# An adaLN attention block on one core: 1/sigma broadcast through a DRAM row, scale parts by column tiles

## The chip, the cores and the metric

The kernel runs on one core of a Trainium2 chip. The metric is device time in microseconds (us) of one execution. The kernel before was run three times: 97.16 us in the median (97.13 to 97.92). The profile that this text reads is one further execution.

## The reference

Only these lines matter; `x` is 2 x 256 x 1152, all data bf16.

```python
mod = (_silu(c) @ w_mod).reshape(B, 6, 1, D)
shift_a, scale_a, gate_a, shift_m, scale_m, gate_m = [mod[:, i] for i in range(6)]
h = _layernorm(x, axis=-1) * (1 + scale_a) + shift_a
qkv = h @ wqkv
q, k, v = (qkv[..., :D].copy(), qkv[..., D:2 * D].copy(), qkv[..., 2 * D:].copy())
p = _softmax(jnp.einsum('bqd,bkd->bqk', q, k) * D ** (-0.5), axis=-1)
a = jnp.einsum('bqk,bkd->bqd', p, v) @ wo
return x + gate_a * a
```

So there are three modulation rows of 1152 values for each of the two batch entries (shift, scale, gate), a layer norm over 1152 columns, the three projections, attention over 256 keys with a single head, and the gated output projection.

## The kernel before, in words

**Layout.** The 512 tokens are four tiles of 128 (`t` = 0..3), the 1152 model columns nine tiles of 128 (`k` = 0..8). `x` is loaded with tokens on partitions, centred by its mean, and turned by TensorE (PE) into `xcT[k]`: model columns on partitions, 512 tokens along the row. All engines' instructions go through a recorder (`_Rec`), which is why nearly every line of the profile says L85, and at the end each engine's instructions, DMA issues included, are pinned to the order in which the program wrote them. What an engine does next is thus set by hand.

**Scale and normalisation are split.** `hTs[k] = xcT[k] * (1 + scale)` needs only the scale row; 1/sigma is multiplied in later. For K this is enough: a key's 1/sigma is applied to the scores in the end (`scores`, line 540), and the shift's share of K adds the same amount to all scores of a query, which the softmax drops. So the K projection starts from `hTs`, before the variances are known, and Q and V use `hT[k] = hTs[k] * rstd_bc + shift`, where `rstd_bc` is 1/sigma of the 512 tokens on all 128 partitions. `normalised(k)` (line 424) is the multiply on VectorE (DVE), `shifted(i)` (line 469) adds the shift row, two of three on DVE and one of three on ScalarE (ACT).

**Scale parts.** The scale row is computed in parts `PA`, `PB`, `PC` of the nine column tiles (line 41), as their weights `wS` arrive. `scale_rows` (line 270) makes the 128 columns of `wS` the stationary operand and silu(c), repeated to 32 columns, the moving one, so the result lies with model columns on partitions; `scale_out` adds 1 and `scaled_b` makes `hTs`. Every part costs nine matmuls for each of its column tiles. The shift row (lines 460 to 467) is made the other way round: silu(c) is the stationary operand of 32 columns, the weights `wH` move, and four matmuls each fill 32 PSUM partitions (a column tile of the array each); a DVE 32x32 block transpose then brings the columns to the partitions.

**K projection.** `accs[0..4]` are five PSUM banks that hold K's column tiles 0 to 4 while `k_step(k)` adds one row tile after the other. Tiles 5 to 8 have no bank of their own: their first two row tiles are computed early by `pair_part`, parked in `held` by `park`, and the rest comes in `held_block(i, ...)`, with `add_held(i)` adding the two on DVE. The named banks `pa`, `pb`, `pc` are shared by `psS`, the pairs, the transposes, `psK` and `psH`.

**1/sigma.** Variances come from DVE's batch-norm statistics for tiles 0 and 3 and from ACT's squares for 1 and 2; GpSimd (POOL) gathers them in `var` and takes the power -1/2 (lines 405 to 408). To bring `rstd` from one value per partition to a row on all partitions it is split in three bf16 parts, turned by PE (`pT3`), multiplied by a 12-row mask on DVE (`masked`), summed over the 12 rows by a matmul against ones (`bc_ps`) and copied to `rstd_bc` by ACT. This chain stands between the K steps on PE, and the nine `normalised` multiplies on DVE stand right behind it.

**Loads.** All weights are issued by SyncE (SP) in one order: `x`, parts of `wS`, the nine row tiles of `wK`, `wH`, `wQ`, `wG`, the rest of `wQ`, `wV`, `wO`. ACT issues only the load of `c` and the last store.

**The end.** In the output projection the last 192 columns of the last token tile use weights already multiplied by the gate (`wo_last`). The nine multiplies `gated_columns` are shared: `ONPOOL` = 4 on POOL (line 608), the other five on DVE, one after each chunk of the output from the fourth chunk on. DVE also does two operations for each chunk (`ga`, `o_sb`), and the last stores wait for its `o_sb`.

Of the kernel before, what the change touches and what calls it, by code (L numbers as in the profile page):

```python
# [16 lines left out]
def kernel(  # L17
# [20 lines left out]

    NACC = 5
    NPARK = KT - NACC  # L40
    PA, PB, PC = (0, 2), (2, 5), (5, KT)
    KA = PA[1]
    NR = 32

# [10 lines left out]
    work = ctx.enter_context(tc.tile_pool(name="work", bufs=2))  # L55
    const = ctx.enter_context(tc.tile_pool(name="const", bufs=1))
    small = ctx.enter_context(tc.tile_pool(name="small", bufs=4))
    psum = ctx.enter_context(tc.tile_pool(name="psum", bufs=5, space=PSUM))
    psum_a = ctx.enter_context(tc.tile_pool(name="psum_a", bufs=1, space=PSUM))
    psum_b = ctx.enter_context(tc.tile_pool(name="psum_b", bufs=1, space=PSUM))  # L60
# [5 lines left out]
    def bank(shape, name, dtype=None, where=None):  # L66
        if where is None:
            where = ring[turn_no[0] % len(ring)]
            turn_no[0] += 1
        return where[0].tile(shape, dtype or F32, tag=where[1], name=name)  # L70
# [39 lines left out]
    def one(t):  # L110
        return slice(t * P, (t + 1) * P)
# [8 lines left out]
    )  # L120
    neg_half = const.tile([P, TT], F32)
    gps.memset(neg_half, -0.5)
    NP3 = 3 * TT
    mask = const.tile([NP3, TT, P], BF16)

    gps.memset(mask, 1.0)
    gps.affine_select(
        out=mask, in_=mask, compare_op=ALU.is_ge, fill=0.0, base=0,
        pattern=[[-3, TT], [0, P]], channel_multiplier=1,
    )  # L130
    gps.affine_select(
        out=mask, in_=mask, compare_op=ALU.is_ge, fill=0.0, base=2,
        pattern=[[3, TT], [0, P]], channel_multiplier=-1,
    )

    c_sb = const.tile([P, B, KT], BF16)
    x_sb = act.tile([P, TT, D], BF16)
    sca.preload_act_table_set("natural_log_exp_and_others")
# [17 lines left out]
    def load_k(k0, k1, c0=0, c1=D):  # L156
        spq.dma_start(out=wK[:, k0:k1, c0:c1], in_=wqkv_v[:, k0:k1, D + c0 : D + c1])
# [21 lines left out]
    load_s(PC, 0, 4)  # L179
    load_s(PC, 4, KT)  # L180
    load_k(5, 6)
    load_k(6, 7)
    load_k(7, KT)
    for k0, k1 in ((0, 3), (3, 6), (6, KT)):
# [23 lines left out]


    mean = const.tile([P, TT], F32)  # L210
    var = const.tile([P, TT], F32)
    rstd = const.tile([P, TT], F32)
    nmean = const.tile([P, TT], F32)
    xc = act.tile([P, TT, D], BF16, tag="a1")
# [6 lines left out]
    def bn(t, after_second=None):  # L221
        st = small.tile([P, NCH, 6], F32, tag="stats", name="stats")
        for s in range(NCH):
            bn_part(t, st, s)
            if s == 1 and after_second is not None:
                after_second()
        mv = small.tile([P, 2], F32, tag="mv", name="mv")
        vec.bn_aggr(out=mv, in_=st)
        return mv

    def act_mean(t):
        sca.activation(out=xc[:, t, :], in_=x_sb[:, t, :], func=ACT.Copy, accum_out=ssum[t])
        sca.activation(out=nmean[:, t : t + 1], in_=ssum[t], func=ACT.Copy, scale=-1.0 / D)

    def act_var(t):
        sca.activation(out=xc[:, t, :], in_=x_sb[:, t, :], func=ACT.Square, bias=nmean[:, t : t + 1],
                       scale=1.0, accum_out=ssum[t])
        gps.tensor_scalar_mul(out=var[:, t : t + 1], in0=ssum[t], scalar1=1.0 / D)

    def centre(t, scalar, op, c0=0, c1=D):  # L240
        vec.tensor_scalar(out=xc[:, t, c0:c1], in0=x_sb[:, t, c0:c1], scalar1=scalar, scalar2=None, op0=op)
# [4 lines left out]
    def transposes(t, h, where):  # L246
        k0, k1 = HALF[h]
        tp = bank([P, 5, P], "tp", BF16, where)
        for k in range(k0, k1):
            ten.transpose(tp[:, k - k0, :], xc[:, t, k * P : (k + 1) * P], ident)  # L250
        tps[t, h] = tp
# [18 lines left out]
    def scale_rows(part, kk0, kk1, js=None, where=None):  # L270
        if kk0 == 0:
            psS[part] = bank([P, part[1] - part[0], NR], "psS", where=where)
        for j0, j1 in [part] if js is None else js:
            for kk in range(kk0, kk1):
                for j in range(j0, j1):
                    ten.matmul(psS[part][:, j - part[0], :], lhsT=wS[:, kk, j * P : (j + 1) * P], rhs=sc_rhs(kk),
                               start=(kk == 0 and j == part[0]), stop=(kk == KT - 1), skip_group_check=True)

    def scale_out(part):
        vec.tensor_scalar_add(out=s1p[:, part[0] : part[1], :], in0=psS[part][:, :, 0:B], scalar1=1.0)  # L280

    def scaled(k, sl, scalar):
        vec.tensor_scalar(out=hTs[:, k, sl], in0=xcT[:, k, sl], scalar1=scalar, scalar2=None, op0=ALU.mult)

# [4 lines left out]
    def scaled_b(k, b):  # L289
        scaled(k, tok(b), s1p[:, k, b : b + 1])  # L290
# [4 lines left out]
    def k_part(k, sl):  # L295
        for f in range(NACC):
            ten.matmul(accs[f][:, sl], lhsT=wk(k, f), rhs=hTs[:, k, sl],
                       start=(k == 0 and sl.start == 0), stop=False, skip_group_check=True)
# [7 lines left out]
            ten.matmul(ps[:, i, :], lhsT=wk(k, f0 + i), rhs=hTs[:, k, sl],  # L306
                       start=(k == 0 and i == 0), stop=(k == KA - 1), skip_group_check=True)

    def park(pr):
        ps, f0, sl = pr  # L310
        sca.copy(out=held[:, f0 - NACC : f0 - NACC + 2, sl], in_=ps)

    def k_step(k, f0=0, f1=NACC):
        for f in range(f0, f1):
            ten.matmul(accs[f], lhsT=wk(k, f), rhs=hTs[:, k, :],
                       start=False, stop=(k == KT - 1), skip_group_check=True)
# [9 lines left out]
    def add_held(i):  # L326
        vec.tensor_tensor(out=qkT[:, KT + NACC + i, :], in0=psK[i], in1=held[:, i, :], op=ALU.add)

    def evac(on_dve, out_ap, in_ap):
        if on_dve:  # L330
            return vec.tensor_copy(out=out_ap, in_=in_ap)
        return sca.copy(out=out_ap, in_=in_ap)


    fillers(12)
    sca.activation(out=e_sb, in_=c_sb, func=ACT.Exp, scale=-1.0)
    gps.tensor_scalar_add(out=e_sb, in0=e_sb, scalar1=1.0)
    mv0 = bn(0, after_second=silu_c)
    centre(0, mv0[:, 0:1], ALU.subtract)
    act_mean(1)  # L340
    centre(1, nmean[:, 1:2], ALU.add)
    act_mean(2)
    transposes(0, 0, MM)
    transposes(0, 1, MM)
    xcT_copy(0, 0, True)
# [45 lines left out]
    st3 = small.tile([P, NCH, 6], F32, tag="stats", name="stats")  # L391
    bn_part(3, st3, 0)
    act_var(1)
    for k in range(KA):
        k_part(k, one(3))
    scale_rows(PB, 0, KT, where=BA)
    scale_out(PB)
    for k in range(*PB):
        for b in range(B):
            scaled_b(k, b)  # L400
    bn_part(3, st3, 1)
    bn_part(3, st3, 2)
    mv3 = small.tile([P, 2], F32, tag="mv", name="mv")
    vec.bn_aggr(out=mv3, in_=st3)
    pr11, pr21 = pair(0, 1, BB), pair(1, 1, BC)
    for pr in (pr11, pr21):
        for k in range(KA):
            pair_part(pr, k)
        park(pr)
    act_var(2)  # L410
    gps.tensor_copy(out=var[:, 0:1], in_=mv0[:, 1:2])
    gps.tensor_copy(out=var[:, 3:4], in_=mv3[:, 1:2])
    gps.tensor_scalar_add(out=rstd, in0=var, scalar1=EPS)
    gps.tensor_tensor(out=rstd, in0=rstd, in1=neg_half, op=ALU.pow)
    for k in range(*PB):
        k_step(k)


    scale_rows(PC, 0, KT, where=BB)
    scale_out(PC)  # L420
    for k in range(*PC):
        for b in range(B):
            scaled_b(k, b)
    parts = const.tile([P, TT, 3], BF16)
    rest = const.tile([P, TT], F32)
    gps.tensor_copy(out=parts[:, :, 0], in_=rstd)
    gps.tensor_tensor(out=rest, in0=rstd, in1=parts[:, :, 0], op=ALU.subtract)
    gps.tensor_copy(out=parts[:, :, 1], in_=rest)
    gps.tensor_tensor(out=rest, in0=rest, in1=parts[:, :, 1], op=ALU.subtract)
    gps.tensor_copy(out=parts[:, :, 2], in_=rest)  # L430
    held_block(0, PB, BA)
    k_step(PC[0])
    k_step(PC[0] + 1, 0, 1)
    pT3 = bank([NP3, P], "pT3", BF16, BC)
    ten.transpose(pT3, parts.rearrange("p t i -> p (t i)"), ident)
    masked = const.tile([NP3, TT, P], BF16)
    vec.tensor_tensor(out=masked, in0=pT3.unsqueeze(1).to_broadcast([NP3, TT, P]), in1=mask, op=ALU.mult)
    k_step(PC[0] + 1, 1)
    bc_ps = bank([P, T], "bc_ps", where=BC)
    ten.matmul(bc_ps, lhsT=junk[:NP3, :P], rhs=masked.rearrange("p t n -> p (t n)"), start=True, stop=True)  # L440
    sca.copy(out=rstd_bc, in_=bc_ps)

    def normalised(k):
        vec.tensor_tensor(out=hT[:, k, :], in0=hTs[:, k, :], in1=rstd_bc, op=ALU.mult)

    for k in range(KT):
        normalised(k)
    for k in range(PC[0] + 2, KT):
        k_step(k)
    for f in range(NACC):  # L450
        evac(False, qkT[:, KT + f, :], accs[f])

    held_block(0, PC)
    held_block(1, (KA, KT), BC)
    held_block(2, (KA, KT), MM)
    add_held(0)
    add_held(1)


    psH = bank([P, KT, 32], "psH", where=BB)  # L460
    wH_v = wH.rearrange("p kk (k j c) -> p kk k j c", k=KT, j=4)
    for kk in range(KT):
        for j in range(4):
            ten.matmul(psH[32 * j : 32 * j + 32], lhsT=sc_rhs(kk), rhs=wH_v[:, kk, :, j, :],
                       start=(kk == 0), stop=(kk == KT - 1))
    shT = const.tile([P, KT, 32], F32)
    vec.transpose(out=shT.rearrange("p k c -> p (k c)"), in_=psH.rearrange("p k c -> p (k c)"))

# [9 lines left out]
    for i in range(KT * B):  # L478
        shifted(i)
    held_block(3, (KA, KT), BA)  # L480
    add_held(2)
    add_held(3)

    def wq(k, f):
        return wQ[:, k, f * P : (f + 1) * P]
# [119 lines left out]
        eng.tensor_tensor(out=wo_last[:, k, :], in0=wO[:, k, D - TAILW :],  # L605
                          in1=gate_bc[:, B - 1, D - TAILW :], op=ALU.mult)

    ONPOOL = 4
    for k in range(KT - ONPOOL, KT):
        gated_columns(gps, k)  # L610

# [85 lines left out]
```

## Time and profile before

| | |
|---|---|
| median of the runs | 97.16 us |
| the profiled execution's own time | 97.31 us |
| its span (first to last instruction) | 95.6 us |
| PE busy | 90.3 us (94% of the span), 661 matmuls |
| DVE busy | 69.4 us (73%) |
| ACT busy | 35.0 us (37%) |
| POOL busy | 23.2 us (24%) |
| TensorE clock granted | 1.000 |
| moved by DMA | 21.31 MB; the DMA engines are filled from about 2.5 to 52 us |

An entry of the time line gives the start in us from the span's start, the time that the merged instructions cover, the engine, the operation, output and input, how many there are, and in brackets how long the engine was idle before and what ended that. Matmuls overlap, so the step from one to the next is shorter than the duration of one. The time of 97.31 us is 1.7 us longer than the span; that part lies outside the instructions.

### The profile page before, as it was taken

Reading aid. Unit: us, or ns where it says so; the run is one execution under the profiler, and the core shown is the slowest. Engines: PE = TensorE matmul, PEld = TensorE weight load, DVE = VectorE, ACT = ScalarE, POOL = GpSimd, SP = SyncE. Lnnn points to the kernel's source line nnn. Section 1 sums busy time; section 2 is a strip of 40 time slices with the busy share of each in tenths; the row PEclk is TensorE's granted clock in tenths of the full one; section 3 lists DMA queues with packets and bytes.
Section 4 is the critical chain, followed back from the end, with each engine's and each line's share of the span. In section 5 each row is a group of like instructions: output and inputs, shape, how many; then the busy total and the mean of one; then the engine's idle time right before and its main releaser. Section 6 shows DMA issues by size and latency. Waiting matters only on the chain.

```text
span 95.6 us, 1687 instructions
## 1 busy us (share of the span) xinstructions
PE 90.3 (94%) x661; PEld 53.9 (56%) x665; DVE 69.4 (73%) x132; ACT 35.0 (37%) x73; POOL 23.2 (24%) x30
## 2 busy tenths in 40 slices
PE   3999999899999999999999999999999999999960
PEld 1349994633445444444458666556678656656660
DVE  2478868073999979999974899991018487999970
ACT  5197689002820900642330489233246300000020
POOL 5520002740000000000000000007999990018000
PEclk9999999999999999999999999999999999999999
DMA  2999999999999999999999102110000000311041
GB/s 28 336 328 358 372 401 380 408 414 408 406 404 411 412 410 412 385 372 371 391 413 409 73 0 52 36 29 0 0 0 0 0 0 0 130 67 57 10 185 52
DMA packets 16023, 21.31 MB, mean 223 GB/s; under 512 B 2192, under 2 KB 9360, under 8 KB 16016
## 3 DMA queue, kind: packets, MB, share of 16 engines
q1 hardware_dynamic: 15600, 21.19, 60.2%
q8 instruction: 5, 0.08, 0.3%
q10 hardware_dynamic: 416, 0.02, 0.3%
q14 instruction: 2, 0.02, 0.0%
HBM read 19.76 MB, written 1.18 MB: 219 GB/s over the span
## 4 chain that ended last, share of the span: by engine, by line
PE 76%; DMA 15%; SPq 3%; DVE 1%; issue 1%; ACT 0%
PE ps L85 41%; PE psQ L85 18%; DMA wS<-in_w_mod_dram 10%; PE psK L85 6%; DMA x_sb<-in_x_dram 5%; PE acc L85 5%; PE s_ps L85 4%; SPq L85 3%; PE psH L85 1%; PE psS L85 1%; DVE hTs L85 1%; PE bc_ps L85 0%; ACT o_sb L85 0%; DVE s1p L85 0%; PE pT L85 0%
## 5 line engine op out<-in xcount | busy, mean ns | idle before, releaser
L85 POOL PARTITION_ALL_REDUCE gate_bc<-gacc x2 | 13.7, 6886 | 44.5 <-DVE gacc L85 44.5
L85 DVE SCALAR_TENSOR_TENSOR gacc<-wG,scT_f,gacc 128x1152 f32<-128x1152 bf16 x16 | 22.4, 1416 | 0.4
L85 PE MATMUL ps<-wV,hT 128*128 128x384 bf16 x108 | 17.7, 326 | 0.0
L85 PE MATMUL psQ<-hT,wQ 128*128 128x512 bf16 x80 | 17.6, 379 | 0.1
L85 PE MATMUL ps<-wO,attnT 128*128 128x384 bf16 (+2 forms) x108 | 17.0, 319 | 0.0
L85 PEld LDWEIGHTS <-attnT 128*128 128x128 bf16 x126 | 11.4, 98 | 6.3
L85 PEld LDWEIGHTS <-hT 128*128 128x128 bf16 x108 | 10.6, 98 | 6.9
L85 PEld LDWEIGHTS <-wK 128*128 128x128 bf16 x109 | 9.5, 97 | 7.6 <-issue 1.0
L85 PEld LDWEIGHTS <-wQ 128*128 128x128 bf16 x81 | 7.9, 98 | 9.5
L85 PE MATMUL acc<-hTs,wK 128*128 128x512 bf16 (+2 forms) x64 | 11.0, 312 | 0.2
L85 ACT CAST qkT<-psQ 128x512 bf16<-128x512 f32 x9 | 5.0, 592 | 11.7 <-PE psQ L85 11.1
L85 DVE CAST attnT<-ps 128x512 bf16<-128x512 f32 (+1 forms) x6 | 3.5, 602 | 6.8 <-PE ps L85 6.8
L85 ACT CAST v_sb<-ps 128x384 bf16<-128x384 f32 x12 | 5.5, 475 | 7.9 <-PE ps L85 7.9
L85 DVE TENSOR_TENSOR ga<-ps,gate_bc 128x384 f32<-128x384 f32 (+2 forms) x12 | 6.4, 536 | 2.1 <-PE ps L85 2.0
L85 DVE TENSOR_TENSOR o_sb<-ga,x_sb 128x384 bf16<-128x384 f32 (+2 forms) x12 | 7.1, 595 | 0.4
L85 PE MATMUL junk_ps<-junk 128*128 128x512 bf16 x12 | 5.3, 632 | 1.5 <-DVE junk L85 1.5
L85 ACT CAST o_sb<-ps 128x128 bf16<-128x128 f32 (+1 forms) x2 | 0.5, 239 | 17.0 <-DVE ga L85 17.0
L85 DVE TENSOR_TENSOR hT<-hTs,held 128x512 bf16<-128x512 bf16 x9 | 5.5, 682 | 1.5 <-ACT held L85 1.5
L85 PE MATMUL psK<-hTs,wK 128*128 128x512 bf16 x26 | 6.3, 379 | 0.1
L85 DVE BATCH_NORM_STATS2 stats<-x_sb 128x6 f32<-128x384 bf16 x6 | 3.1, 541 | 2.2 <-DMA x_sb<-in_x_dram 2.2
L85 PEld LDWEIGHTS <-junk 128*128 128x128 bf16 (+1 forms) x13 | 1.7, 140 | 4.7 <-issue 3.2
L85 POOL TENSOR_TENSOR wo_last<-wO,gate_bc 128x192 bf16<-128x192 bf16 x4 | 2.5, 651 | 6.8 <-issue 6.8
(74 smaller groups left out, 89.7 us busy)
## 6 DMA issues: line engine op xcount, KB each, us to landing
wH<-in_w_mod_dram SPq DMA_DIRECT2D x3, 864.0 KB, 11.7
wG<-in_w_mod_dram SPq DMA_DIRECT2D x3, 864.0 KB, 12.7
wV<-in_wqkv_dram SPq DMA_DIRECT2D x3, 864.0 KB, 13.3
wO<-in_wo_dram SPq DMA_DIRECT2D x3, 864.0 KB, 8.7
wK<-in_wqkv_dram SPq DMA_DIRECT2D x7, 288.0 KB, 7.1
wQ<-in_wqkv_dram SPq DMA_DIRECT2D x3, 576.0 KB, 12.7
x_sb<-in_x_dram SPq DMA_DIRECT2D x4, 288.0 KB, 3.6
wQ<-in_wqkv_dram SPq DMA_DIRECT2D x1, 864.0 KB, 12.7
```

The costliest lines, as they stand in the source:

```text
L85: r = fn(*a, **k)
```

## The change

1/sigma no longer passes through PE. POOL computes `rstd` straight from the variances (now one tile `mvs`, which bn_aggr and ACT's squares write in place), ACT stores it to a DRAM row of 512 values, and a second DMA, issued by ACT as well, reads the row back to all 128 partitions (`rstd_all`, 128 x 2048 bytes); ACT copies it to `rstd_bc`, in another order of its elements. The mask, the three parts, `pT3`, `masked` and `bc_ps` go.

`PC` is cut in two (`PC` = tiles 5 and 6, `PD` = 7 and 8), with the loads of `PD` behind the load of wK's row tile 5. `PB`, `PC` and `PD` are computed by column tiles as the shift row is, with a DVE transpose each (`scale_tiles`, `scale_turned`); they stand at other places between the K steps. The shift row is made in two pieces with `held_block(2)` between them. One of the four parks and two of the five evacuations of `accs` move from ACT to DVE. The nine `normalised` move behind those evacuations and `add_held(0)`; `add_held(1)` moves behind `shifted`. `ONPOOL` becomes 2.

```diff
-    PA, PB, PC = (0, 2), (2, 5), (5, KT)
+    PA, PB, PC, PD = (0, 2), (2, 5), (5, 7), (7, KT)
...
     load_k(5, 6)
+    load_s(PD, 0, 4)
+    load_s(PD, 4, KT)
     load_k(6, 7)
...
     def act_var(t):
-        sca.activation(out=xc[:, t, :], in_=x_sb[:, t, :], func=ACT.Square, bias=nmean[:, t : t + 1],
-                       scale=1.0, accum_out=ssum[t])
-        gps.tensor_scalar_mul(out=var[:, t : t + 1], in0=ssum[t], scalar1=1.0 / D)
+        sca.activation(out=xc[:, t, :], in_=x_sb[:, t, :], func=ACT.Square, bias=snm[:, t : t + 1],
+                       scale=float(D) ** -0.5, accum_out=mvs[:, t, 1:2])
...
+    wS_v = wS.rearrange("p kk (k j c) -> p kk k j c", k=KT, j=4)
+    sT = const.tile([P, KT, 32], F32)
+    def scale_tiles(part, where):
+        psS[part] = bank([P, part[1] - part[0], 32], "psS", where=where)
+        for kk in range(KT):
+            for j in range(4):
+                ten.matmul(psS[part][32 * j : 32 * j + 32], lhsT=sc_rhs(kk), rhs=wS_v[:, kk, part[0] : part[1], j, :],
+                           start=(kk == 0), stop=(kk == KT - 1))
+    def scale_turned(part):
+        vec.transpose(out=sT[:, part[0] : part[1], :].rearrange("p k c -> p (k c)"),
+                      in_=psS[part].rearrange("p k c -> p (k c)"))
+        vec.tensor_scalar_add(out=s1p[:, part[0] : part[1], :], in0=sT[:, part[0] : part[1], 0:B], scalar1=1.0)
...
-    for k in range(KA):
-        k_part(k, one(3))
-    scale_rows(PB, 0, KT, where=BA)
-    scale_out(PB)
+    k_part(0, one(3))
+    scale_tiles(PB, BA)
+    k_part(1, one(3))
+    scale_turned(PB)
...
-        park(pr)
+        park(pr, on_dve=(pr is pr21))
     act_var(2)
-    gps.tensor_copy(out=var[:, 0:1], in_=mv0[:, 1:2])
-    gps.tensor_copy(out=var[:, 3:4], in_=mv3[:, 1:2])
-    gps.tensor_scalar_add(out=rstd, in0=var, scalar1=EPS)
+    gps.tensor_scalar_add(out=rstd, in0=mvs[:, :, 1], scalar1=EPS)
     gps.tensor_tensor(out=rstd, in0=rstd, in1=neg_half, op=ALU.pow)
-    for k in range(*PB):
-        k_step(k)
-    scale_rows(PC, 0, KT, where=BB)
-    scale_out(PC)
+    rstd_row = dram.tile([P, TT], F32, name="rstd_row")
+    rstd_all = const.tile([P, P, TT], F32)
+    sca.dma_start(out=rstd_row, in_=rstd)
+    sca.dma_start(out=rstd_all.rearrange("q p t -> q (p t)"),
+                  in_=rstd_row.rearrange("p t -> (p t)").partition_broadcast(P))
+    k_step(2)
+    k_step(3)
+    k_step(4, 0, 2)
+    scale_tiles(PC, BB)
+    scale_turned(PC)
     for k in range(*PC):
         for b in range(B):
             scaled_b(k, b)
...
+    k_step(4, 2)
     held_block(0, PB, BA)
-    k_step(PC[0])
-    k_step(PC[0] + 1, 0, 1)
-    pT3 = bank([NP3, P], "pT3", BF16, BC)
-    ten.transpose(pT3, parts.rearrange("p t i -> p (t i)"), ident)
...
-    bc_ps = bank([P, T], "bc_ps", where=BC)
-    ten.matmul(bc_ps, lhsT=junk[:NP3, :P], rhs=masked.rearrange("p t n -> p (t n)"), start=True, stop=True)
-    sca.copy(out=rstd_bc, in_=bc_ps)
+    k_step(5)
+    k_step(6, 0, 2)
+    scale_tiles(PD, BB)
+    scale_turned(PD)
+    for k in range(*PD):
+        for b in range(B):
+            scaled_b(k, b)
+    k_step(6, 2)
+    held_block(0, PC)
+    sca.copy(out=rstd_bc.rearrange("q (t p) -> q t p", p=P), in_=rstd_all.rearrange("q p t -> q t p"))
...
+    for k in range(*PD):
+        k_step(k)
+    for f in range(NACC):
+        evac(f < 2, qkT[:, KT + f, :], accs[f])
+    held_block(0, PD)
+    add_held(0)
     for k in range(KT):
         normalised(k)
-    for k in range(PC[0] + 2, KT):
-        k_step(k)
-    for f in range(NACC):
-        evac(False, qkT[:, KT + f, :], accs[f])
-    held_block(0, PC)
     held_block(1, (KA, KT), BC)
-    held_block(2, (KA, KT), MM)
-    add_held(0)
-    add_held(1)
...
+    shift_tiles(0, 6)
+    held_block(2, (KA, KT), MM)
+    shift_tiles(6, KT)
...
     held_block(3, (KA, KT), BA)
-    add_held(2)
-    add_held(3)
+    for i in (1, 2, 3):
+        add_held(i)
...
-    ONPOOL = 4
+    ONPOOL = 2
```

More of the change, by code (lines that the diff above doesn't have):

```diff
@@ L57 @@
     small = ctx.enter_context(tc.tile_pool(name="small", bufs=4))
+    dram = ctx.enter_context(tc.tile_pool(name="dram", bufs=1, space=bass.MemoryType.DRAM))
     psum = ctx.enter_context(tc.tile_pool(name="psum", bufs=5, space=PSUM))
@@ L122 @@
     gps.memset(neg_half, -0.5)
[L123 to L134, printed above, removed]
     c_sb = const.tile([P, B, KT], BF16)
@@ L210 @@
     mean = const.tile([P, TT], F32)
-    var = const.tile([P, TT], F32)
+    mvs = const.tile([P, TT, 2], F32)
+    snm = const.tile([P, TT], F32)
     rstd = const.tile([P, TT], F32)
@@ L226, in bn @@
                 after_second()
-        mv = small.tile([P, 2], F32, tag="mv", name="mv")
-        vec.bn_aggr(out=mv, in_=st)
-        return mv
+        vec.bn_aggr(out=mvs[:, t, :], in_=st)
     def act_mean(t):
@@ L307, in pair_part, with evac, park @@
                        start=(k == 0 and i == 0), stop=(k == KA - 1), skip_group_check=True)
-    def park(pr):
+    def evac(on_dve, out_ap, in_ap):
+        if on_dve:
+            return vec.tensor_copy(out=out_ap, in_=in_ap)
+        return sca.copy(out=out_ap, in_=in_ap)
+    def park(pr, on_dve=False):
         ps, f0, sl = pr
-        sca.copy(out=held[:, f0 - NACC : f0 - NACC + 2, sl], in_=ps)
+        evac(on_dve, held[:, f0 - NACC : f0 - NACC + 2, sl], ps)
     def k_step(k, f0=0, f1=NACC):
@@ L327, in add_held @@
         vec.tensor_tensor(out=qkT[:, KT + NACC + i, :], in0=psK[i], in1=held[:, i, :], op=ALU.add)
[L329 to L332, printed above, removed]
     fillers(12)
@@ L337 @@
     gps.tensor_scalar_add(out=e_sb, in0=e_sb, scalar1=1.0)
-    mv0 = bn(0, after_second=silu_c)
-    centre(0, mv0[:, 0:1], ALU.subtract)
+    bn(0, after_second=silu_c)
+    centre(0, mvs[:, 0, 0:1], ALU.subtract)
     act_mean(1)
@@ L342 @@
     act_mean(2)
+    gps.tensor_scalar_mul(out=snm[:, 1:3], in0=nmean[:, 1:3], scalar1=float(D) ** -0.5)
     transposes(0, 0, MM)
@@ L402 @@
     bn_part(3, st3, 2)
-    mv3 = small.tile([P, 2], F32, tag="mv", name="mv")
-    vec.bn_aggr(out=mv3, in_=st3)
+    vec.bn_aggr(out=mvs[:, 3, :], in_=st3)
     pr11, pr21 = pair(0, 1, BB), pair(1, 1, BC)
@@ L423 @@
             scaled_b(k, b)
[L424 to L430, printed above, removed]
-    held_block(0, PB, BA)
-    k_step(PC[0])
-    k_step(PC[0] + 1, 0, 1)
-    pT3 = bank([NP3, P], "pT3", BF16, BC)
@@ L435 @@
-    ten.transpose(pT3, parts.rearrange("p t i -> p (t i)"), ident)
-    masked = const.tile([NP3, TT, P], BF16)
-    vec.tensor_tensor(out=masked, in0=pT3.unsqueeze(1).to_broadcast([NP3, TT, P]), in1=mask, op=ALU.mult)
-    k_step(PC[0] + 1, 1)
-    bc_ps = bank([P, T], "bc_ps", where=BC)
-    ten.matmul(bc_ps, lhsT=junk[:NP3, :P], rhs=masked.rearrange("p t n -> p (t n)"), start=True, stop=True)
-    sca.copy(out=rstd_bc, in_=bc_ps)
+    k_step(4, 2)
+    held_block(0, PB, BA)
+    k_step(5)
+    k_step(6, 0, 2)
@@ L446, with shift_tiles @@
+    held_block(0, PD)
+    add_held(0)
     for k in range(KT):
         normalised(k)
-    for k in range(PC[0] + 2, KT):
-        k_step(k)
-    for f in range(NACC):
-        evac(False, qkT[:, KT + f, :], accs[f])
-    held_block(0, PC)
     held_block(1, (KA, KT), BC)
-    held_block(2, (KA, KT), MM)
-    add_held(0)
-    add_held(1)
     psH = bank([P, KT, 32], "psH", where=BB)
     wH_v = wH.rearrange("p kk (k j c) -> p kk k j c", k=KT, j=4)
[L462 to L465, printed above, removed]
+    def shift_tiles(kk0, kk1):
+        for kk in range(kk0, kk1):
+            for j in range(4):
+                ten.matmul(psH[32 * j : 32 * j + 32], lhsT=sc_rhs(kk), rhs=wH_v[:, kk, :, j, :],
+                           start=(kk == 0), stop=(kk == KT - 1))
```

## The prediction, made before the change was run

> **What bounds the kernel now.** I read the page's shares first (PE busy 90.3 of 95.6 us at clock 1.00), then the chain of waits around the edited stretch (start, us, what):
>
> ```profile
> 18.56 0.68 PE psS L85 x20
> 19.26 0.18 DVE s1p L85
> 19.46 0.49 DVE hTs L85 x2
> 20.00 1.46 PE acc L85 x6
> 21.45 0.15 PE pT L85
> 21.60 0.97 PE acc L85 x4
> 22.57 0.32 PE bc_ps L85
> ...
> 29.04 1.22 PE psH L85 x36
> ```
>
> From 20.00 us on every link but the last copy and store is PE work, so a step of PE saved ahead of psQ is a gain, provided psQ's operand hT is ready by then. The time line tells when that is:
>
> ```profile
> 17.87 1.06 POOL L85 TENSOR_TENSOR rstd<-rstd,neg_half 128x4 f32<-128x4 f32 x1
> 22.93 0.58 ACT L85 COPY held<-bc_ps 128x512 f32<-128x512 f32 x1 [6.02 <-PE bc_ps L85]
> 23.55 5.50 DVE L85 TENSOR_TENSOR hT<-hTs,held 128x512 bf16<-128x512 bf16 x9 [1.49 <-ACT held L85]
> 30.31 0.48 DVE L85 STREAM_TRANSPOSE shT<-psH 128x288 f32<-128x288 f32 x1
> 30.83 2.44 DVE L85 TENSOR_SCALAR hT<-hT,shT 128x256 bf16<-128x256 bf16 x12
> 31.71 17.65 PE L85 MATMUL psQ<-hT,wQ 128*128 128x512 bf16 x80
> ```
>
> The nine multiplies (0.60 from one to the next) end at 29.05, before psH does. hT's first row tile needs two shifts (0.20 to the next start, 0.28 long), so it stands at 31.3, 0.4 us ahead of psQ. DVE has no more slack than that.
>
> **PE.** Steps between matmuls by the time line: 0.2155 us at 512 columns, 0.115 at 256, 0.055 at 128. In scale_rows a step is 0.025 (27 in 0.83, less the last one's 0.18): 0.68 for PB, 0.91 for PC. Gone are these 1.59, pT3 (21.30 to 21.54: 0.24), bc_ps (22.40 to 22.82: 0.42), and two waits: for wS (16 psS from 17.75 end at 18.15, the next starts at 18.55: 0.40) and for hTs (the other 20 end at 19.07 and three psK at 19.73, the next starts at 20.00: 0.27).
>
> No column tiles of 64 or 96 columns are in the trace; the nearest row is psH with 288. How many psH matmuls were in flight in each stretch (after the comma, in brackets):
>
> ```profile
> 28.98:29.09 0.11, 0.11 (x4) 0.00 (x0) 1.00 1.00 398
> ...
> 29.11:29.22 0.10, 0.10 (x8) 0.00 (x0) 1.00 1.16 461
> 29.22:29.24 0.02, 0.02 (x12) 0.00 (x0) 1.00 0.87 346
> ```
>
> Four start together and the next four 0.12 us later, which is the streaming of 288 columns at 0.42 ns. By columns a set of four costs 0.043 at 96 and 0.029 at 64, so nine sets 0.38 for PB and 0.26 each for PC and PD. Going into psH loses 0.09 (28.97 after a psK at 28.66) and leaving it 0.10, so each group pays 0.19. Three groups: 0.90 + 0.57 = 1.47, hardly less than the 1.59. The upper bound is 0.025 a matmul as in scale_rows, 0.90 a group.
>
> New waits on PE. scale_tiles(PB) takes the bank of pr20, whose park ends at 12.86, and now stands ahead of k_part(1): 0.30 lost. Loads: in the stretch with wS in pieces of 512 bytes (5.0 to 7.5 us) 339 GB/s moved, around PC (15.0 to 18.5) 393. PC's 1.18 MB landed at 18.51, so began near 15.5; as two halves of 1.74 us with wK5 (0.72) between, they land at 17.25 and 19.7, and wK6 at 20.4 in place of 19.9 (issued 11.63, 8.3 to landing).
>
> Walk from 12.36 (k_part(0) of token tile 3): five matmuls 0.28, wait 0.30, PB 0.57, five 0.28, the eight of the pairs 0.92 (14.70); 12 K steps 2.59 (17.29, PC just there); PC 0.45; 11 steps 2.37 (20.11); wait for wK6 0.3; two steps 0.43; PD 0.45; 17 steps 3.66. held_block(0, PD) is issued by 24.95, its result there at 25.1. The hTs of each part hide behind the steps between (PB: transpose 0.26 by 1.04 ns a column, add 0.17, two hTs 0.48: 14.45, needed at 14.70); the park moved to DVE, 0.6, fits in its pause before PC (2.82 us now, until the psS that feed s1p). After that: 7 steps 1.51, six shift sets 0.93, 7 steps, three sets 0.56, 7 steps: PE is ready for psQ at 31.0; wH, 0.5 late from the small pieces and 0.65 from the 256 KB of rstd_all, adds 0.2: 31.2. PE alone would gain 0.5 us.
>
> **hT, where the time goes.** Two things must be there for the first multiply. add_held(0) ends at 25.1 + 0.60 = 25.7 (the two evacuations on DVE, 0.6 each from 23.85, fit ahead). And rstd_bc: ACT's squares end at 16.91 as before; POOL saves its scaling and copies (16.99 to 17.54), so rstd stands near 18.4 in place of 18.93. ACT, with nothing else to do then (idle 6.02 in the row above), waits on POOL, stores, waits for the landing, loads, waits, copies 0.59; behind these waits are queued only three evacuations of accs, needed for banks at psQ. Neither DMA has a row of its own kind. ACT's load of c (4.5 KB, beside x's loads) took 3.0, the last store 1.8: I take 3.0 for the 2 KB row, as it too runs beside full queues. For 256 KB: the store's 1.8 plus 1.3 at half of 400 GB/s gives 3.1; wS of 256 KB took 4.4:
>
> ```profile
> wS<-in_w_mod_dram SPq DMA_DIRECT2D x1, 256.0 KB, 4.4
> c_sb<-in_c_dram ACTq DMA_DIRECT2D x1, 4.5 KB, 3.0
> out_dram<-o_sb ACTq DMA_DIRECT2D x1, 16.0 KB, 1.8
> ```
>
> I take 4.3, c's 3.0 plus the 1.3, near the row. Bounds: 1.8 + 3.1 = 4.9 below, hidden; above, SP's loads in this stretch took 12.7 each, but they stood in SP's own queue. So 18.45 + 3.0 + 0.05 + 4.3 + 0.05 + 0.59 = 26.45, 0.75 behind add_held(0). Nine multiplies 5.42 (31.87), transpose to first shift 0.52, two shifts 0.48: hT's first tile at 32.9, psQ at 32.95. That is 1.25 later than now, and PE idles 1.7 of it. Behind psQ everything to the projection is PE-bound as now; gates have room (DVE waited 1.83 for s_ps).
>
> **The end.** DVE takes two more wo_last multiplies, POOL two fewer. At the end of DVE's work:
>
> ```profile
> 85.63 0.93 DVE L85 TENSOR_TENSOR o_sb<-ga,x_sb 128x384 bf16<-128x384 f32 x1
> 86.49 0.70 DVE L85 TENSOR_TENSOR wo_last<-wO,gate_bc 128x192 bf16<-128x192 bf16 x1
> ...
> 92.20 0.42 DVE L85 TENSOR_TENSOR o_sb<-ga,x_sb 128x256 bf16<-128x256 f32 x1
> 92.73 0.37 ACTq L660 DMA_DIRECT2D out_dram<-o_sb  x1
> ```
>
> A chunk with its multiply costs DVE 1.46, exactly PE's 1.47; without, 1.06. While POOL works (85.61 to 88.11) DVE lags 0.76 more, and catches up by the last chunk (0.15 behind). Two more multiplies are 0.80; halving POOL's 2.5 us gives back 0.25, since the slowest two of DVE's operations (0.93, 0.70) lie in its first half. So the last o_sb ends 0.55 later; SP's store behind it had 0.15 to spare against ACT's (landing 94.4 and 94.53): 0.4 to 0.45 on the end.
>
> Sum on the profiled execution: 97.31 + 1.25 + 0.42 = 99.0. The median of the runs lies 0.15 below that execution, so 98.9.
>
> A page speaks against the narrow tiles: the Trainium skill, "TensorEngine Tiling (Array Packing)", Performance Considerations, says each matmul carries some 60 cycles, so that one column takes as long as 60. The four psH that begin together are against it for column tiles; no run here has narrower ones.
>
> **The rivals.**
> 1. *The row is hidden.* DMAs on ACT's queue cost the lower bounds; add_held(0) then sets the start at 25.7 and psQ 32.2: 0.75 less, 98.15. For it: ACT's queue is empty. Chance 0.22.
> 2. *The row queues with the backlog.* If each of the two also waits for what the 16 engines hold, as every SP load does, each us goes on the end in full; at 5 and 6 us in place of 3.0 and 4.3, 3.7 more: 102.6. Against it: c's load landed in 3.0 beside x's 3.6. Chance 0.13.
> 3. *Narrow column tiles run at 0.025 a matmul.* Then the three groups cost 1.80 more, of which 0.3 covers wK6's wait: the first multiply at 27.2, psQ at 33.7, 99.7. For it: scale_rows does run at that step. Chance 0.05. The 60 cycles of that page of the Trainium skill, 25 ns by an estimate, would give this case.
> 4. *Not slower.* Groups change without loss and the loads are in time: 0.57 + 0.30 + 0.3 less, held_block(0, PD) at 23.8, add_held(0) at 24.5. With rstd_bc by then (both DMAs at 4.9 in all: 24.0) hT stands at 30.9, psQ at PE's 31.0 at the latest, and if POOL's half share frees DVE wholly (0.76 against 0.80), the end adds nothing: 96.5. It decides when rstd_bc and add_held(0) are both there before 24.9. Chance 0.12, mostly half way, 96.5 to 98.
>
> **How the numbers follow.** Forecast 98.9 with chance 0.48, its own range 98.3 to 99.6. The range leaves out the better end of rival 4 and the worse half of rival 2: 97.5 to 100.8. About 1% (96.2 to 98.1) is what a measurement can tell from no change. Within it lie rival 4 but for a few hundredths, and half of rival 1: 0.22. Faster 0.03, slower 0.75.
>
> **What would show it.** Right: PE idle for 1 to 2 us ahead of the first psQ, released by DVE's hT; ACT waiting for rstd_all; the multiplies starting near 26.4. ACT's two DMAs give 3.0 and 4.3 or other values. psS sets 0.04 and 0.03 apart. The last o_sb some 0.5 further behind its matmuls. Wrong: psQ following held_block(3) without idle time, or the first multiply released by add_held(0).

## The result, and the profile after

The changed kernel takes 104.52 us in the median of four runs (104.05 to 105.47); the kernel before, on the same chip, 97.33. The ratio is 1.074, with a 95% interval of 1.069 to 1.078. It is 7.2 us slower where 1.6 to 1.7 were forecast, and outside the range of 97.5 to 100.8. The profiled execution has a span of 102.6 us (before 95.6).

The chain of waits around the edited stretch, to be held against the one of before:

```profile
16.60 0.24 POOL rstd L86
16.92 1.07 POOL rstd L86
18.01 4.94 DMA rstd_row<-rstd
...
23.03 6.52 DMA rstd_all<-rstd_row
...
29.57 1.13 ACT held L86
...
30.73 5.51 DVE hT L86 x9
36.23 0.40 DVE shT L86
...
36.66 0.52 ACT hT L86
...
37.28 8.30 PE psQ L86 x30
45.64 10.74 PE psQ L86 x49
56.43 4.09 PE s_ps L86 x36
```

Between 18 and 37 us no link is PE's any more. Two DMAs take 11.5 us, one after the other, then come ACT's copy and the nine multiplies. The same stretch in the time line, where the brackets show what the engines stood idle for:

```profile
29.57 1.12 ACT L86 COPY held<-rstd_all 128x512 f32<-128x512 f32 x1 [13.20 <-DMA rstd_all<-rstd_row]
30.73 5.51 DVE L86 TENSOR_TENSOR hT<-hTs,held 128x512 bf16<-128x512 bf16 x9 [4.84 <-ACT held L86]
...
37.28 8.09 PE L86 MATMUL psQ<-hT,wQ 128*128 128x512 bf16 x29 [6.07 <-ACT hT L86]
```

PE has done all its work ahead of psQ by 31.2 us and then stands for 6.07. Now psQ: the chain gives 30 matmuls in 8.30 us, where 0.2155 each would be 6.5. The stretches by windows say why (after the core's busy times and counts, the last three columns are the granted clock, the DMA share and GB/s):

```profile
30.90:37.20 6.30, 0.32 (x2) 0.00 (x0) 6.26 (x13) 1.79 (x5) 0.00 (x0) 0.74 1.04 410
37.28:40.70 3.42, 3.42 (x9) 1.19 (x10) 3.42 (x13) 1.88 (x5) 0.00 (x0) 0.50 1.04 405
40.70:44.00 3.30, 3.30 (x17) 1.53 (x16) 3.23 (x4) 0.00 (x0) 0.00 (x0) 1.00 1.09 374
```

While PE stands idle its clock falls to half, and it stays there for the first 3.4 us of psQ: 9 matmuls in flight in that time against 17 in the next 3.3 us.

The 7.0 us of span are therefore three items. psQ starts at 37.28 in place of 31.71: 5.57. From the first psQ to the first ps go 23.25 us (to 60.53) in place of 21.58 (31.71 to 53.29): 1.67. The end, from the last copy's start to the end of the span, takes 0.2 less (102.6 - 99.72 = 2.9 in place of 95.6 - 92.48 = 3.1).

### The profile page after: what moved, and what is told of

It reads as the page before. It is cut to its first block, busy times and chain, and to the rows that moved or that the text cites. A ratio compares the mean times of both kernels' runs of the same rounds, so it can differ in the third digit from the quotient of the medians.

```text
span 102.6 us, 1771 instructions
## 1 busy us (share of the span) xinstructions
PE 91.0 (89%) x702; PEld 52.9 (52%) x708; DVE 71.8 (70%) x140; ACT 34.0 (33%) x70; POOL 18.6 (18%) x17
## 4 chain that ended last, share of the span: by engine, by line
PE 63%; DMA 17%; DVE 9%; SPq 3%; ACT 2%; POOL 1%; issue 1%; ACTq 0%; POOLq 0%
PE ps L86 38%; PE psQ L86 19%; DMA rstd_all<-rstd_row 6%; DMA wK<-in_wqkv_dram 6%; DVE hT L86 5%; DMA rstd_row<-rstd 5%; PE s_ps L86 4%; SPq L86 3%; ACT held L86 2%; POOL rstd L86 1%; DVE hTs L86 1%; PE acc L86 1%; DVE stats L86 1%; PE psE L86 1%; PE psS L86 1%
## 5 line engine op out<-in xcount | busy, mean ns | idle before, releaser
L86 PE MATMUL psQ<-hT,wQ 128*128 128x512 bf16 x79 | 19.0, 404 | 6.1 <-ACT hT L86 6.1
L86 PE MATMUL acc<-hTs,wK 128*128 128x512 bf16 (+2 forms) x64 | 11.6, 313 | 0.7 <-DMA wK<-in_wqkv_dram 0.4
L86 DVE TENSOR_TENSOR o_sb<-ga,x_sb 128x384 bf16<-128x384 f32 (+2 forms) x12 | 6.5, 541 | 0.4
L86 ACT COPY held<-rstd_all 128x512 f32<-128x512 f32 x1 | 1.1, 1120 | 13.2 <-DMA rstd_all<-rstd_row 13.2
L86 PE MATMUL s_ps<-qkT 128*128 128x256 bf16 x36 | 4.1, 273 | 0.1
## 6 DMA issues: line engine op xcount, KB each, us to landing
wG<-in_w_mod_dram SPq DMA_DIRECT2D x3, 864.0 KB, 12.7
```

Of the source, the lines that this page charges most:

```text
L86: r = fn(*a, **k)
```

## The experiments

**Row by PE, all else as changed.** The first question is whether the two DMAs are the whole of it.

```diff
-    sca.dma_start(out=rstd_row, in_=rstd)
-    sca.dma_start(out=rstd_all..., in_=rstd_row....partition_broadcast(P))
+    (mask, parts, pT3, masked, bc_ps and its copy, as in the kernel before;
+     pT3 within k_step(5), bc_ps ahead of scale_tiles(PD))
```

> The changed kernel with 1/sigma brought to the row by PE as in the kernel before (three bf16 parts, transpose, mask, matmul against ones), the multiplies still behind add_held(0) and all else as changed. If the two DMAs are the whole cause: the first multiply waits for add_held(0) only and starts near 26.4 us, psQ near 32.8, no clock drop, 98.3 us (97.9 to 98.8). If other parts of the change cost more than 1 us as well: 99.5 or more. If the order of the multiplies costs nothing either: 97.3.

Measured: 98.29 us, ratio 1.010 (1.007 to 1.014). The time line:

```profile
25.70 0.69 DVE L86 TENSOR_TENSOR qkT<-psK,held 128x512 bf16<-128x512 f32 x1
26.30 5.49 DVE L86 TENSOR_TENSOR hT<-hTs,held 128x512 bf16<-128x512 bf16 x9
...
32.86 11.38 PE L86 MATMUL psQ<-hT,wQ 128*128 128x512 bf16 x51 [1.19 <-ACT hT L86]
```

The multiplies follow add_held(0) without a gap, psQ comes at 32.86 with 1.19 us of idle time ahead of it, and its matmuls keep the step of 0.2155 us (51 in 11.38) at a granted clock of 1.00. So the row's way through DRAM costs 6.2 of the 7.2 us (104.52 against 98.29, both beside the same kernel before at 97.33), and 1.0 us is left for the rest of the change.

**PE kept busy while it waits.** How much of the 6.2 is the clock?

```diff
+    for _ in range(27):
+        ten.matmul(q_acc[0], lhsT=junk[:, :P], rhs=junk, start=True, stop=True)
     for k in range(KT):
         for f in range(QACC):
             ten.matmul(q_acc[f], lhsT=wq(k, f), rhs=hT[:, k, :], ...)
```

> The changed kernel with 27 matmuls of ones (5.8 us) in PE's idle time before the first psQ; they write a bank that psQ then overwrites. Clock theory (PE is idle for 6.07 us, the granted clock falls to 0.5 and stays there for the first 3.4 us of psQ): psQ starts where it did, clock 1.00 throughout, 80 psQ in 17.65 us in place of 19.1, the time falls by 1.45 us to about 103.1. Rival (psQ is slow for another reason, such as its weights still arriving by DMA): the psQ steps stay at 0.43 us for the first eight and the time stays at 104.5.

Measured: 102.84 us, ratio 1.059 (1.054 to 1.064). The time line:

```profile
31.28 5.99 PE L86 MATMUL psQ<-junk 128*128 128x512 bf16 x27 [0.36 <-ACT qkT L86]
...
37.25 7.07 PE L86 MATMUL psQ<-hT,wQ 128*128 128x512 bf16 x31
```

and its windows:

```profile
31.20:37.20 6.00, 5.92 (x27) 2.64 (x27) 5.96 (x13) 1.50 (x5) 0.00 (x0) 1.00 1.04 410
37.25:40.70 3.45, 3.40 (x17) 1.56 (x17) 3.45 (x13) 1.96 (x5) 0.00 (x0) 1.00 1.04 401
```

psQ starts where it did, the clock stays at 1.00 there, and 1.7 us are gone, by both the medians and the spans (102.6 to 100.9). Work without any use made the kernel faster. That the clock is the cause of the slow psQ is shown; the expectation of 1.45 left out that s_ps is a little shorter too (3.93 in place of 4.09).

The Trainium skill, "TensorE: Matmul & The Clock Gate", Part 1, says that the clock falls to half after some 3.4 us of idleness and comes back after as much activity. The traces agree with it in size only: in the changed kernel the clock falls 2.6 us into the idle time (at 33.86) and comes back at 40.69, after 3.4 us of psQ; with both DMAs on POOL's queue, a run further down, it comes back after 3.1 us of psQ. In the run with PE's row, 1.19 us of idle time cost no clock. Where the two differ, the traces decide.

**Why the two DMAs take 11.5 us.** Four kernels ask this, each run once; they are read by their traces. First, the same pair a second time near 70 us, when the loads are over, with one copy in the permuted order and one straight:

```diff
+        if gidx == 7:
+            sca.dma_start(out=row2, in_=rstd)
+            sca.dma_start(out=rstd_all..., in_=row2....partition_broadcast(P))
+            sca.copy(out=turned (t p order), in_=rstd_all (permuted))
+            sca.copy(out=flat, in_=rstd_all (as it lies))
```

> The changed kernel with ACT's two DMAs made a second time near 70 us, when the loads are over, and with two ACT copies of the row behind them: one in the permuted order of the change, one in the order in which it lies. Queue theory (the two landings of 4.94 and 6.52 us are long because the engines are full of SP's loads): about 1.8 to 2.2 us for the 2 KB store and 2.4 to 3.0 us for the 256 KB load, of which about 1.5 us from issue to the first packet in place of 3.9. Kind theory (16-byte writes to DRAM, and 128 reads of the same 2 KB, are slow by themselves): again near 4.9 and 6.5 us. Copies: 1.1 us permuted and 0.6 us straight if the order of the elements costs; both 1.1 us if a source in SBUF costs. The time of the whole stays within 1 us of the changed kernel's.

The DMA issues in the windows of the second pair (KB, us to landing), and ACT's copies:

```profile
rstd_row<-rstd ACTq DMA_DIRECT2D x1, 2.0 KB, 1.4
rstd_all<-rstd_row ACTq DMA_DIRECT2D x1, 256.0 KB, 4.3
```

```profile
80.47 1.13 ACT L86 COPY turned<-rstd_all 128x512 f32<-128x512 f32 x1 [5.29 <-DMA rstd_all<-rstd_row]
81.50 0.62 ACT L86 COPY flat<-rstd_all 128x512 f32<-128x512 f32 x1
```

The store falls from 4.9 to 1.4 us, clearly the queue theory. The load falls only to 4.3, between the two. The copy's 1.1 us are the order of its elements (16 bytes apart in the source), not SBUF as a source. The time of the whole, 107.62 us, missed its expectation of 1 us. Most of that lies ahead of the second pair: the first pair took 5.38 and 7.17 us in this run, psQ started at 38.98 in place of 37.28 and ran longer at half clock, and the first ps came at 62.97 in place of 60.53. Only some 0.7 us lie behind it, where ACT, which evacuates PE's results, stood for 5.3 us behind the DMA.

Second, to split the 4.3: a plain load of 256 KB from 128 different rows, early beside SP's loads and late alone, and behind the late one the broadcast again.

```diff
+    sca.dma_start(out=plain, in_=x_f[0:P, 0 : 8 * P])        # near 10 us
...
+            sca.dma_start(out=plain, in_=x_f[0:P, 0 : 8 * P])    # near 72 us
+            sca.dma_start(out=rstd_all..., in_=rstd_row....partition_broadcast(P))
```

> The changed kernel with three more DMAs on ACT's queue: a plain 256 KB load (128 different rows of x, 2048 bytes each) near 10 us beside SP's loads, the same load again near 70 us with the queues empty, and behind it a second broadcast of the 2 KB row. If reading one DRAM row 128 times is what makes the broadcast slow (4.3 us even with empty queues): plain load 2.4 to 3.0 us late, broadcast 4.3 again. If any 256 KB load on ACT's queue takes that: both near 4.3. Early plain load: 5 us or more if the full engines cost about 2 us as they did for the row.

The issues in three windows, in order of time:

```profile
plain<-in_x_dram ACTq DMA_DIRECT2D x1, 256.0 KB, 5.4
...
plain<-in_x_dram ACTq DMA_DIRECT2D x1, 256.0 KB, 2.7
rstd_all<-rstd_row ACTq DMA_DIRECT2D x1, 256.0 KB, 3.2
```

The full engines cost a plain load 2.7 us, as the queue theory has it. Alone, the broadcast takes 0.5 us longer than a plain load; the 4.3 of the run before did not come back, so there is no fixed price of reading one row 128 times. What differed there is that the row had just been written; that this is the reason is not shown.

The packet records of ACT's queue show where the time under load goes. From the issue to the first packet it is 3.5 us for the store (18.01 to 21.53) and for the broadcast (23.03 to 26.54) of the changed kernel, and 3.6 for the early plain load. Alone it is 0.8 for the store, 1.0 for the plain load and for the broadcast, and 2.1 for the broadcast right behind its store. (The 3.9 in the expectation of the late pair has the 0.4 us from the last packet to the landing in it.) The packets themselves, once begun, last 1.0 us for the row and 2.6 for the broadcast under load, 0.2 and 1.9 alone. So most of what the load of the engines costs is a wait ahead of the first packet. What makes that wait, no run shows.

Third, both DMAs from POOL's queue.

```diff
-    sca.dma_start(out=rstd_row, ...)      -    sca.dma_start(out=rstd_all, ...)
+    gps.dma_start(out=rstd_row, ...)      +    gps.dma_start(out=rstd_all, ...)
```

> The changed kernel with both DMAs issued by POOL in place of ACT. If the wait is one of the 16 engines' shared time, the landings stay near 5 and 6.5 us and the time near 104.5. If the wait is one in front of ACT's and SP's common way of making descriptors, POOL's own way avoids it: about 2.5 and 3.9 us, the row 5 us earlier, psQ near 33 us and 98.9 us.

Measured: 6.6 and 6.3 us, 105.78 us in all. POOL's queue is no way round the wait: the first packets come 4.1 and 3.8 us after the issue. The profile lists SP's and ACT's queues as `hardware_dynamic` and POOL's as `software_dynamic`, so a wait that only the first kind meets does not explain this by itself. What POOL's queue costs beside empty engines no run shows, so a wait of its own could hide here.

Fourth, in place: SP's loads from wH on held back until the row has landed.

```diff
+    for kk in (0, 3, 6):
+        gps.tensor_copy(out=wH[:, kk, 0:1], in_=rstd_all[:, 0, 0:1])
     (the loads of wH and of wQ's first three pieces, moved here)
```

> The changed kernel with SP's loads of wH and all that follow held back until rstd_all has landed (POOL writes one element of the row into each piece of wH ahead of its load, and the load overwrites it), so that the engines run empty once wK is in, near 22 us. Queue theory: the store, still beside the last of wK, 3 to 5 us; the broadcast load, with empty queues, 3.2 to 4.3 us in place of 6.5, its first packet 1.3 to 2.5 us after the issue; ACT's copy near 26 us. Kind theory: 6.5 us again. The time of the whole rises, since wH and wQ come later: 106 or more.

```profile
17.95 4.04 DMA rstd_row<-rstd
...
22.01 3.24 DMA rstd_all<-rstd_row
```

In the chain of this run the store, still beside the last of wK, takes 4.04, and the broadcast, with the engines empty, 3.24 in place of 6.52. The multiplies begin at 26.43, 4.3 us earlier. The whole gains nothing from it (104.95, where I expected 106 or more): wH now comes late, PE waits for it, 4.00 us and then 1.45, its clock is at 0.50 from 31.5 to 38.4, and psQ starts at 39.5. So the load of the engines by SP's own transfers is the cause of half of the 11.5 us or rather more: 3.3 of the broadcast's 6.52 went here, in place, and 3.5 of the store's 4.94 in the run with the late pair. It cannot simply be taken away.

**The last 1.0 us.** In the run with PE's row the multiplies stand behind add_held(0), as in the change. Here they stand ahead of the last K steps again, and all five evacuations are ACT's (in the kernel before, `normalised` is at line 443, not 424):

```diff
     for k in range(KT):
         normalised(k)
     for k in range(*PD):
         k_step(k)
     for f in range(NACC):
-        evac(f < 2, qkT[:, KT + f, :], accs[f])
+        evac(False, qkT[:, KT + f, :], accs[f])
     held_block(0, PD)
     add_held(0)
```

> The kernel of the run te_row (row by PE, all else as changed) with the nine multiplies back ahead of the last K steps and all five evacuations of accs on ACT, as before the change. Order theory (the 1.2 us by which psQ starts late in te_row is the multiplies' place behind add_held(0)): multiplies from about 22.7 us, hT's first tile near 31, psQ follows PE's own work at 31.7 and the time is that of before, 97.3 (97.0 to 97.6). Rival (the column tiles and the three parts of the scale row cost PE as much): psQ still near 32.8 with no idle time ahead of it, 98.3.

Measured: 96.73 us, ratio 0.992 (0.990 to 0.995): 0.7 us less than the kernel before, and better than the 97.3 that I expected. The time line:

```profile
23.20 5.50 DVE L86 TENSOR_TENSOR hT<-hTs,held 128x512 bf16<-128x512 bf16 x9
...
30.08 1.69 PE L86 MATMUL psK<-hTs,wK 128*128 128x512 bf16 x7
...
31.61 1.67 PE L86 MATMUL psQ<-hT,wQ 128*128 128x512 bf16 x7
```

psQ follows PE's own work without idle time, at 31.61 against 32.86 with the multiplies behind add_held(0) and 31.71 before. So the 1.0 us was the order of the multiplies, with the two evacuations that moved along with them; column tiles, the three parts and the shift row in two pieces cost PE nothing on balance. Of the 0.7 us gained on the kernel before, the profiled executions show 0.1 in psQ's start and 0.2 behind the last copy; where the rest lies they do not show.

Two further kernels pad the transpose and the row matmul to the whole array, the second with three gated multiplies on POOL.

```diff
-    ten.transpose(pT3, parts (12 columns), ident)
+    ten.transpose(pT3, parts_full (128 columns, the others zero), ident)
-    ten.matmul(bc_ps, lhsT=junk[:NP3, :P], rhs=masked (12 rows), ...)
+    ten.matmul(bc_ps, lhsT=junk[:, :P], rhs=masked (128 rows, the others zero), ...)
```

> As hybrid, but the transpose of the three bf16 parts and the matmul against ones use all 128 rows and columns of the array, padded with zeros. If the 0.24 and 0.42 us that pT3 and bc_ps cost PE come from changing the array's tiling in and out (12 columns, 12 rows), about 0.3 us less than hybrid: 97.0. If they come from the two instructions themselves, the same as hybrid within 0.1.

> As hybrid_full (whole-array transpose and row matmul), with three gated multiplies on POOL in place of two. In the profile of hybrid_full psQ starts 0.25 us earlier than in hybrid, but the chain at the end runs over DVE's last o_sb. If DVE's seven multiplies hold up the end there, one less brings the 0.25 out: 96.5 (96.3 to 96.7). If POOL's third multiply slows DVE as much as it saves, 96.7 to 96.9 as before.

Measured: 96.78 us for both, ratios 0.992 (0.989 to 0.995) and 0.993 (0.990 to 0.996). They cannot be told from the run before them. In the first of the two, the matmul behind the transpose starts 0.06 us after it in place of 0.16, but the next one waits for wK6 until 20.39, so some of what is saved goes into that load. Whether the tiling is the cause of the price of pT3 and bc_ps stays open. The expected gain of the third multiply did not come: psQ starts at 31.55 in that run, where the one before had 31.36.

**Two gated multiplies on POOL, alone in the kernel before.**

```diff
-    ONPOOL = 4
+    ONPOOL = 2
```

> The kernel before with two of the nine gated multiplies on POOL in place of four, nothing else. The prediction's term: DVE ends 0.55 us later and the time rises by 0.42 to 97.75. Rival (DVE's slowing beside POOL is worth as much as the two multiplies, as the changed kernel's end suggests): 97.1 to 97.4, within 0.2 of before, o_sb's last end at most 0.1 us later behind its matmuls.

Measured: 97.31 us, ratio 0.999 (0.996 to 1.001): no change. At the end of DVE's work in this run:

```profile
87.33 0.70 DVE L85 TENSOR_TENSOR o_sb<-ga,x_sb 128x384 bf16<-128x384 f32 x1
...
92.37 0.43 DVE L85 TENSOR_TENSOR o_sb<-ga,x_sb 128x256 bf16<-128x256 f32 x1
92.42 0.51 ACT L85 CAST o_sb<-ps 128x128 bf16<-128x128 f32 x2 [17.02 <-PE ps L85]
```

Only one of DVE's operations is slow beside POOL (0.70), and the last o_sb ends with ACT's copies as before.

## Why the prediction was wrong, point by point

**PE's part was right.** The walk put the end of add_held(0) at 25.7 and PE's readiness for psQ at 31.2; it ended at 25.9 (25.19 and 0.69) and PE was done at 31.2. The sets of column tiles, priced by psH, cost what was said: the 36 of PB lie within 0.57 us, 0.043 from set to set, and at 64 columns 36 take 0.46 us, 0.029 from set to set or 0.007 a matmul. Rival 3 (0.025 a matmul) is refuted. The Trainium skill, "TensorEngine Tiling (Array Packing)", Performance Considerations, gives some 60 cycles for each matmul. Taken for each column tile by itself, as rival 3 did with its estimate of 25 ns, that does not hold here; as a least time for a whole set of four these runs cannot test it, since no set here takes less than 0.029.

**The mechanism was right.** hT is late because of the row, PE stands idle ahead of psQ, and what is queued behind ACT's waits costs nothing of its own.

**The step that failed is the term of the two landings.** It had 3.0 + 4.3 us; they were 4.94 + 6.52, 4.2 more (in the four runs that make them alike, 4.9 to 5.6 and 6.2 to 7.2). Rival 2 had the size (5 and 6, 102.6 us) and got 0.13. The store was priced by ACT's load of c at the span's start, and I called the queues full there; they were only beginning to fill when that load was issued, at 0.7 us (the page gives 48 GB/s in the first of its 40 slices after the change, 28 before). The rows that were in the state of this stretch were SP's, at 12.7 us, and I set them aside as standing in SP's own queue. The runs show that a DMA of another queue does not stand behind all of that but does wait 2.5 to 2.7 us longer for its first packet than it does alone, each time. The early plain load (5.4) is the row that the prediction lacked.

**ACT's copy** was taken as 0.59 from the copy of bc_ps; at 16 bytes between its elements it took 1.12. rstd itself was ready 0.4 earlier than I had it (18.0 against 18.4). Together the first multiply stood at 30.73 in place of 26.45, 4.3 late.

**The clock was left out.** PE's idle time was forecast as 1.7 us, and at 1.19 the run with PE's row shows no loss. At 6.07 the clock fell and cost 1.67 more. A long wait on PE has a second price, and rival 2 should have had it. No one length at which it starts can be read off: with the loads held back, PE's wait of 4.00 us still ended at clock 1.00, and the fall came in the wait of 1.45 that followed 0.55 us later.

**The end** was forecast 0.42 later; it was 0.2 earlier, and alone the edit changes nothing. The sum took back only 0.25 of DVE's slowing beside POOL; all of DVE's slow operations but one went away (0.70 for a multiply that takes 0.35 elsewhere), so the 0.55 by which DVE was to end later did not come.

With the measured terms in place the sum closes: 99.0 + 4.3 (first multiply) + 1.67 (clock) - 0.6 (the end) = 104.4, the profiled execution's own 104.44.

## What to carry to other kernels

A small transfer through DRAM in the middle of a phase that fills the DMA engines is priced by a transfer issued in that same phase from a second queue, not by one from the span's start; here each cost about 5 us or more, and the second waits for the first. Where a change lets TensorE wait, ask how long: one of 6 us cost its own length and 1.7 us more at half clock, which useless matmuls in the gap brought back. And when a long operand chain is moved behind an engine's other work, its place in the order can cost more than the work: with 1/sigma's row made by PE, putting nine multiplies back ahead turned a kernel 1% slower than the one before into one 0.8% faster.

## What the runs showed that was not expected

Three quite different DMAs (2 KB store, 256 KB broadcast, 256 KB plain load) each waited 3.5 to 3.6 us from issue to the first packet while SP's loads filled the engines, and 0.8 to 1.0 us without these. The clock fell in five of the runs: in four of them 2.6 to 5.3 us after PE's last matmul ahead of psQ, in the fifth (loads held back) in the second of two waits. Each time it stayed at 0.50 for 6.83 us, so how much of that psQ pays for depends on when psQ begins: 3.1 to 4.9 us in the four. An ACT copy of 128x512 f32 took 1.13 us with its source elements 16 bytes apart and 0.62 us with them side by side. Sets of four column tiles of 64 columns started 0.029 us apart.
